# All work emitted by a list scheduler in the kernel, with tiles of its own for attention

## The chip, the cores and the metric

One core of a Trainium2 chip. The metric is device time in microseconds of one execution of the whole program; lower is better. The kernel before takes 993.18 us (median of 3 runs, 992.31 to 993.94).

## The reference, cut to what matters

```python
def _attn_ref(q, k, v, g_norm):                 # 4 batches, 8 heads, 576 tokens, 64 wide
    kv = np.einsum('bhsd,bhse->bhde', k, v)
    out = np.einsum('bhsd,bhde->bhse', q, kv)
    rms = np.sqrt(np.mean(out * out, axis=-1, keepdims=True) + 1e-06)
    return out / rms * g_norm

def _moe_ref(x, w_a, w_b, w_out):               # x 2304 x 512, inner width 1536
    return (x @ w_a) * (x @ w_b) @ w_out

def _moe2_ref(x, w_gate, w_val, w_out):
    gate = 1.0 / (1.0 + np.exp(-(x @ w_gate)))
    return gate * (x @ w_val) @ w_out
```

Attention without softmax, then two expert layers on the 2304 tokens, all in float32. Weights arrive as float64 bits (64-bit words) and are made float32 on the chip.

## The kernel before, in words

**Attention.** There are 18 tiles of 128 tokens. For each of the 4 batches four loads bring keys and values, 20 matmuls give the product of keys and values for all heads (word K in the order FIRST), and two copies put it into a block-diagonal tile (V). For each tile of tokens: a load of queries (D), the product with the block-diagonal tile into a bank (O), a square on ScalarE and a sum on VectorE (S), the reciprocal root on GpSimd for three tiles at once (R, `powers`, a scale-and-add and a power instruction of 24 columns), the normalisation on VectorE (N), four transposes on TensorE (T) and a scaled copy into `part`, the transposed x (Y). Attention borrows tiles of the expert layers: query tiles lie in those of the gated product, squares and normalised tiles in those of the first products.

**Expert layers.** The tokens are cut into 3 blocks of 768 (j), the inner width into 6 passes of two slices u and v (q), and there are two layers (m): 36 groups (m, q, j). A product of a group is a 256 x 256 by 256 x 384 block product; of these 7 instead of 8 are made from sums and differences of the blocks of x and of the weights (`x_comb`, `w_sums`), and recombined behind TensorE (`after`). They are numbered 1 to 7, for u and v each. Every operand is split into a rounded high part (ScalarE) and the remainder, the low part (a subtraction on GpSimd, in some cases VectorE), and a product is three matmuls for each of two inner halves: six matmuls of 384 columns, called a slot here. The gated product of u and v then goes through `down`, eight slots for a group, whose results VectorE adds into `part` (in the first pass q = 0 they are copied instead, by ScalarE and VectorE in turn).

**x.** In pass q = 0 of each layer the seven x operands of a block are made (`x_comb`), kept in a ring `xr` of 6 tiles and stored to DRAM; in the later passes they are loaded back (`load_x`). The keys and values of attention use the same ring.

**Weights.** Of each slice three matrices (a, b, o) are loaded (ring of 2), made float32 in four stages (`w_float`: two ScalarE instructions, three VectorE instructions, one integer add on GpSimd), combined (`w_sums`) and split (`w_parts`) into rings of 3 (wp0 to wp3) and 4 (wo).

**What sets the order.** Each engine executes in the order in which instructions are emitted, and SP, which issues all DMAs, too. That order is written by hand. FIRST lists attention and the first weights, and stands whole ahead of the first product. Then a loop runs over the groups, and in each over 22 slots (SLOTS: fourteen products and eight d, the down products of the group before). After each product of v the next x is made or loaded (`next_x`), and `hooks` places weight work at fixed slot numbers.

Of the kernel before, what the change touches and what calls it, by code (L numbers as in the profile page):

```python
# [10 lines left out]
F32 = mybir.dt.float32  # L11
F32R = mybir.dt.float32r
# [28 lines left out]
TICKS = len(SLOTS)  # L41
ORDER = "1526743"

W_OF = {"1": (0, 0), "2": (0, 1), "5": (1, 0), "7": (1, 1), "6": (2, 0), "4": (2, 1), "3": (3, 0)}

FIRST = """
L00 L01 L02 L03 C D1 L10 L11 D3 H H K0 V0 L12 L13 O0 S0 O1 S1 wa0 O2 S2 R0 L20 L21 D5 L22 L23 O3 S3 wb0 K1 V1
D7 L32 L33 L30 L31 N0 N1 O4 S4 T0 N2 O5 S5 Y0 R3 T1 Y1 q0 T2 Y2 p00 O6 S6 D10 N3 p10 N4 O7 S7 T3 N5 Y3 K2 T4 Y4 T5 Y5 V2
O8 S8 R6 c wa1 p20 D13 c p30 c O9 S9 wb1 N6 N7 q1 K3 c O10 S10 N8 p01 T6 Y6 T7 Y7 c V3 O11 S11 R9 T8 Y8 c p11
D16 O12 S12 O13 S13 N9 N10 p21 N11 T9 Y9 O14 S14 R12 T10 Y10 T11 Y11 p31 D17 O15 S15 O16 S16 N12 N13 O17 S17 R15
T12 Y12 T13 Y13 N14 N15 T14 Y14 T15 Y15 N16 N17 T16 Y16 T17 Y17
"""
# [3 lines left out]
def attention_then_two_moes(  # L61
# [9 lines left out]
    V, A, G = nc.vector, nc.scalar, nc.gpsimd  # L71

    def pool(name, bufs, on=ctx, **kw):
        return on.enter_context(tc.tile_pool(name=name, bufs=bufs, **kw))

    one = pool("one", 1)
    xr = pool("xr", 6)
    wp = pool("wp", 3)
    wo_p = pool("wo", 4)
    w32_p = pool("w32", 2)  # L80
    raw_p = pool("raw", 2)
    cv = pool("cv", 2)
    tmp = pool("tmp", 2)
    tmp2 = pool("gf", 2)
    xs = pool("xs", 1)
    unit = pool("unit", 1)
    small = pool("small", 2)
    dram = pool("dram", 1, space=DRAM)
    ps_u = pool("ps_u", 1, space=PSUM)
    ps_o = pool("ps_o", 2, space=PSUM)  # L90
# [3 lines left out]
    mhalf = one.tile([P, 3 * H], F32, name="mhalf")  # L94

    part = [one.tile([P, 2, KC, N], F32, name=f"part{j}") for j in range(NJ)]


    def u_tile(tag, shape=(P, N), dtype=F32):
        n = int(np.prod(shape[1:]))  # L100
        t = unit.tile([P, max(n, 512)], dtype, tag=tag, name=tag)[:, :n]
        return t if len(shape) == 2 else t.rearrange("p (a n) -> p a n", a=shape[1])

    kvbd = [u_tile(f"c22{x}", (P, KC, P)) for x in "uv"]


    w_raw, w_32, w_sum, w_pt, wo_pt = {}, {}, {}, {}, {}

    w_order = [(0, "a"), (0, "b"), (1, "a"), (1, "b"), (0, "o"), (1, "o")]
    w_order += [(F, w) for F in range(2, 2 * NF) for w in "abo"]  # L110

    def load_w():
        if not w_order:
            return
        F, which = w_order.pop(0)
        raw = raw_p.tile([P, KC * P], U64, tag="raw", name="wraw")
        nc.sync.dma_start(out=raw, in_=w_all[F // NF, F % NF, "abo".index(which)])
        w_raw[F, which] = raw

    def w_float(F, which, stage):  # L120


        raw = w_raw[F, which]
        words = (raw[0] if isinstance(raw, tuple) else raw).bitcast(U32).rearrange("p (n c) -> p n c", c=2)
        low, up = words[:, :, 0], words[:, :, 1]
        if stage == 0:
            mag = cv.tile([P, KC * P], F32, tag="mag", name="w_mag")
            last = cv.tile([P, KC * P], I32, tag="last", name="w_last")
            A.activation(out=mag, in_=up.bitcast(F32), func=ACTF.Abs, scale=65536.0)  # L129
            A.activation(out=last, in_=low, func=ACTF.Copy, scale=2.0**-29)  # L130
            w_raw[F, which] = raw, mag, last
            return
        raw, mag, last = raw
        bits = mag.bitcast(U32)
        if stage == 1:
            V.tensor_scalar(out=mag, in0=mag, scalar1=LEAST, scalar2=MOST, op0=ALU.max, op1=ALU.min)  # L136
            V.tensor_scalar(out=bits, in0=bits, scalar1=3, scalar2=None, op0=ALU.logical_shift_left)  # L137
        elif stage == 2:
            V.scalar_tensor_tensor(  # L139
                out=bits, in0=up, scalar=0x80000000, in1=bits, op0=ALU.bitwise_and, op1=ALU.bitwise_or  # L140
            )
            load_w()
        else:
            if F not in w_32:
                w_32[F] = w32_p.tile([P, 3, KC * P], F32, tag="w32", name="w32")
            dst = w_32[F][:, "abo".index(which), :].bitcast(I32)
            G.tensor_tensor(out=dst, in0=mag.bitcast(I32), in1=last, op=ALU.add)  # L147
            del w_raw[F, which]

    def w_sums(F, stage):  # L150
        w = w_32[F]
        b2 = w[:, 1, 256:512]
        if stage == 0:
            t13 = tmp.tile([P, 512], F32, tag="tmp", name="t13")
            V.tensor_tensor(out=t13, in0=w[:, 1, :], in1=w[:, 0:2, 0:256], op=ALU.subtract)  # L155
            w_sum[F] = [t13]
        else:
            t13 = w_sum[F][0]
            t24 = tmp.tile([P, 512], F32, tag="tmp", name="t24")
            V.tensor_tensor(out=t24[:, 0:256], in0=b2, in1=t13[:, 0:256], op=ALU.subtract)  # L160
            V.tensor_tensor(out=t24[:, 256:512], in0=w[:, 0, 256:512], in1=t24[:, 0:256], op=ALU.subtract)
            w_sum[F].append(t24)

    def w_parts(F, i, stage, eng=G):

        if i == "o":
            src, n = w_32[F][:, 2, :], 512
        elif i == 0:
            src, n = w_32[F][:, 0, :], 512
        elif i == 3:  # L170
            src, n = w_32[F][:, 1, 256:512], 256
        else:
            src, n = w_sum[F][i - 1], 512
        if stage == 0:
            if i == "o":
                t = wo_pt[F] = wo_p.tile([P, 2, n], F32R, tag="wo", name="wo")
            else:
                t = w_pt[F, i] = wp.tile([P, 2, n], F32R, tag=f"wp{i}", name=f"wp{i}")
            A.activation(out=t[:, 0, :], in_=src, func=ACTF.Copy)  # L179
        else:  # L180
            t = wo_pt[F] if i == "o" else w_pt[F, i]
            eng.tensor_tensor(out=t[:, 1, :], in0=src, in1=t[:, 0, :], op=ALU.subtract)  # L182


    x_dram, x_in = {}, {}
    x_sum = {}

    def x_comb(g, i, eng):

        m, q, j = g  # L190
        x11, x12, x21, x22 = (part[j][:, t, c:c + 2, :] for t in (0, 1) for c in (0, 2))
        if i == "5":
            x_sum[0] = one_x("s12")
            V.tensor_tensor(out=x_sum[0], in0=x21, in1=x22, op=ALU.add)  # L194
        elif i == "6":
            V.tensor_tensor(out=x_sum[0], in0=x_sum[0], in1=x11, op=ALU.subtract)  # L196
        elif i == "7":
            x_sum[1] = one_x("s3")
            V.tensor_tensor(out=x_sum[1], in0=x11, in1=x21, op=ALU.subtract)
        elif i == "3":  # L200
            V.tensor_tensor(out=x_sum[0], in0=x12, in1=x_sum[0], op=ALU.subtract)  # L201
        src = {"1": x11, "2": x12, "4": x22, "7": x_sum.get(1)}.get(i, x_sum.get(0))
        t = x_in[g, i] = xr.tile([P, 2, 2, N], F32R, tag="xr", name="xst")
        A.activation(out=t[:, 0], in_=src, func=ACTF.Copy)  # L204
        eng.tensor_tensor(out=t[:, 1], in0=src, in1=t[:, 0], op=ALU.subtract)  # L205
        d = x_dram[m, j, i] = dram.tile([P, 4 * N], F32, name=f"x{m}{j}{i}")
        nc.sync.dma_start(out=d, in_=t.rearrange("p a c n -> p (a c n)").bitcast(F32))

    def one_x(name):
        return xs.tile([P, 2, N], F32, tag=name, name=name)  # L210

    def load_x(g, i):
        m, q, j = g
        t = x_in[g, i] = xr.tile([P, 2, 2, N], F32R, tag="xr", name="xin")
        nc.sync.dma_start(out=t.rearrange("p a c n -> p (a c n)").bitcast(F32), in_=x_dram[m, j, i])

    groups = [(m, q, j) for m in range(2) for q in range(NQ) for j in range(NJ)]
    x_order = [(g, i) for g in groups for i in ORDER]

    def next_x():  # L220

        if not x_order:
            return
        g, i = x_order.pop(0)
        if g[1]:
            load_x(g, i)
        else:
            x_comb(g, i, V if i in "62" else G)


    kvm, qt = {}, {}

    def load_kv(b, p):

        if b < 2 or p > 1:
            t = xr.tile([P, 4 * N], F32, tag="xr", name="kv")[:, :KJ * 2 * P]
        else:
            t = part[b - 1][:, p].rearrange("p k n -> p (k n)")[:, :KJ * 2 * P]
        nc.sync.dma_start(out=t[:KP], in_=kv_in[b, p])
        kvm[b, p] = t[:KP].rearrange("p (j c e) -> p j c e", j=KJ, c=2)  # L240
# [310 lines left out]
```

## Time and profile before

| what | value |
| --- | --- |
| median of 3 runs | 993.18 us (992.31 to 993.94) |
| the profiled execution's own time | 991.95 us |
| its span | 990.1 us, 14127 instructions |
| TensorE matmul busy | 903.9 us, 91% of the span |
| VectorE (DVE) busy | 581.2 us, 59% |
| ScalarE (ACT) busy | 414.0 us, 42% |
| GpSimd (POOL) busy | 474.0 us, 48% |
| DMA | 256.78 MB, mean 259 GB/s |

How to read it: the span is the profiled execution from its first to its last instruction; its own time contains what lies around the span. Busy shares are means over stages that differ, so the rows below go by stages. In a timeline a row is a start, a duration, the engine, the line of the kernel, the instruction with output and inputs, and in brackets the idle time before it and what ended it. PE is TensorE, DVE is VectorE, ACT is ScalarE, POOL is GpSimd. PEclk is the granted clock as a share of the full one.

### The profile page before, as it was taken

The numbers are of one execution on the slowest core, as the hardware profiler recorded it, in microseconds if no ns is written. First come the engines' busy times: TensorE is split into PE (matmuls) and PEld (weight loads), VectorE is DVE, ScalarE is ACT, GpSimd is POOL, SyncE is SP. The second block draws the span as 40 slices with busy tenths as digits, with TensorE's granted clock in tenths as the row PEclk, the third lists the DMA queues.
The fourth block names the chain that finished last, engine by engine and source line by source line (L and its number), as shares of the span: only waits on it lengthen the run. The fifth ranks groups of instructions, "written<-read, shape, count | busy, mean of one in ns | idle before, by whom it ended". The sixth has DMA issues, their size and how long they took to land.

```text
span 990.1 us, 14127 instructions
## 1 busy us (share of the span) xinstructions
PE 903.9 (91%) x5144; PEld 890.9 (90%) x5144; DVE 581.2 (59%) x989; ACT 414.0 (42%) x805; POOL 474.0 (48%) x387
## 2 busy tenths in 40 slices
PE   6645677899999999999999798999999999999998
PEld 5544667899999999999999787999999999999998
DVE  2373388556566556656657868446566656664444
ACT  2244445453333333433434654554543444543321
POOL 2466377544454344444446786444444444544111
PEclk9777788999999999999999989899999999999999
DMA  8752255787887788778875646788778877877783
GB/s 335 291 202 107 117 190 214 287 305 274 281 310 282 282 290 304 273 263 297 306 270 217 235 193 236 264 313 301 273 259 317 284 272 274 302 268 246 248 275 119
DMA packets 55221, 256.78 MB, mean 259 GB/s; under 512 B 6256, under 2 KB 9328, under 8 KB 55152
## 3 DMA queue, kind: packets, MB, share of 16 engines
q1 hardware_dynamic: 55152, 255.88, 71.1%
q8 instruction: 41, 0.67, 0.3%
q14 instruction: 28, 0.23, 0.1%
HBM read 218.10 MB, written 37.75 MB: 258 GB/s over the span
## 4 chain that ended last, share of the span: by engine, by line
PE 76%; DVE 5%; ACT 2%; issue 1%; POOL 1%; DVEq 0%; ACTq 0%
PE ps_u L330 48%; PE ps_o L379 29%; ACT xst L204 1%; DVE w_mag L139 1%; DVE s L194 1%; POOL xst L205 1%; DVE s L196 1%; DVE w_mag L137 0%; DVE w_mag L136 0%; DVE s L201 0%; ACT w_mag L129 0%; DVE part L390 0%; DVE xst L205 0%; POOL w L147 0%; DVE t L155 0%
## 5 line engine op out<-in xcount | busy, mean ns | idle before, releaser
L330 PE MATMUL ps_u<-xin,wp 128*128 128x384 f32 x2520 | 456.4, 334 | 0.0
L330 PEld LDWEIGHTS ps_u<-xin,wp 128*128 128x128 f32 x2520 | 438.6, 188 | 0.0
L379 PE MATMUL ps_o<-gu,wo 128*128 128x384 f32 x864 | 201.6, 341 | 24.7 <-ACT part L386 8.7
L379 PE MATMUL ps_o<-gv,wo 128*128 128x384 f32 x864 | 199.9, 339 | 0.0
L147 POOL TENSOR_TENSOR w<-w_mag,w_last 128x512 int32<-128x512 int32 x72 | 95.0, 1319 | 210.8 <-DVE w_mag L139 164.4
L390 DVE TENSOR_TENSOR part<-ps_o,part 128x384 f32<-128x384 f32 x240 | 131.1, 554 | 107.0 <-PE ps_o L379 106.9
L379 PEld LDWEIGHTS ps_o<-gu,wo 128*128 128x128 f32 x864 | 155.2, 191 | 31.0 <-DVE part L390 11.4
L379 PEld LDWEIGHTS ps_o<-gv,wo 128*128 128x128 f32 x864 | 157.0, 191 | 0.0
L369 POOL TENSOR_TENSOR gu<-gf,gu 128x384 fp32r<-128x384 f32 x72 | 74.6, 1036 | 145.7 <-ACT gu L368 143.8
L330 PE MATMUL ps_u<-xst,wp 128*128 128x384 f32 x504 | 100.8, 357 | 12.4 <-ACT u2u L339 6.7
L330 PEld LDWEIGHTS ps_u<-xst,wp 128*128 128x128 f32 x504 | 96.7, 206 | 13.7 <-ACT u2u L339 7.1
L182 POOL TENSOR_TENSOR wp<-t,wp 128x512 fp32r<-128x512 f32 x48 | 64.7, 1349 | 70.6 <-ACT wp L179 70.6
L368 ACT ACTIVATE gu<-gf 128x384 fp32r<-128x384 f32 x72 | 37.8, 525 | 131.1 <-DVE gf L366 131.1
L369 POOL TENSOR_TENSOR gv<-gf,gv 128x384 fp32r<-128x384 f32 x72 | 77.8, 1081 | 15.9 <-ACT gv L368 13.6
L139 DVE SCALAR_TENSOR_TENSOR w_mag<-wraw,w_mag 128x512 uint32<-128x512 uint32 x72 | 65.2, 906 | 1.2
L136 DVE TENSOR_SCALAR w_mag<-w_mag 128x512 f32<-128x512 f32 x72 | 40.7, 565 | 37.7 <-ACT w_mag L129 36.9
L349 DVE TENSOR_TENSOR c11u<-ps_u,vu 128x384 f32<-128x384 f32 x36 | 20.0, 556 | 57.7 <-PE ps_u L330 57.6
L368 ACT ACTIVATE gv<-gf 128x384 fp32r<-128x384 f32 x72 | 37.6, 523 | 38.3 <-DVE gf L366 36.5
L182 POOL TENSOR_TENSOR wp<-w,wp 128x512 fp32r<-128x512 f32 (+1 forms) x48 | 50.0, 1041 | 6.7 <-ACT wp L179 6.6
L339 ACT ACTIVATE u2u<-ps_u 128x384 f32<-128x384 f32 x36 | 17.6, 489 | 81.1 <-PE ps_u L330 81.1
L129 ACT ACTIVATE w_mag<-wraw 128x512 f32<-128x512 f32 x72 | 47.8, 664 | 6.9 <-DMA wraw<-w_all_dram 5.7
L130 ACT ACTIVATE w_last<-wraw 128x512 int32<-128x512 uint32 x72 | 48.1, 668 | 0.0
(82 smaller groups left out, 865.2 us busy)
## 6 DMA issues: line engine op xcount, KB each, us to landing
xin<-x SPq DMA_DIRECT2D x210, 768.0 KB, 5.6
wraw<-w_all_dram SPq DMA_DIRECT2D x72, 512.0 KB, 4.5
x<-xst SPq DMA_DIRECT2D x42, 768.0 KB, 3.5
kv<-kv_in_dram SPq DMA_DIRECT2D x12, 640.0 KB, 8.3
out_dram<-part SPq DMA_DIRECT2D x24, 192.0 KB, 1.9
part<-kv_in_dram SPq DMA_DIRECT2D x4, 640.0 KB, 7.9
gu<-q_t_dram SPq DMA_DIRECT2D x9, 256.0 KB, 7.5
gv<-q_t_dram SPq DMA_DIRECT2D x9, 256.0 KB, 6.1
```

The lines of the kernel that those rows point to most:

```text
L129: A.activation(out=mag, in_=up.bitcast(F32), func=ACTF.Abs, scale=65536.0)
L130: A.activation(out=last, in_=low, func=ACTF.Copy, scale=2.0**-29)
L136: V.tensor_scalar(out=mag, in0=mag, scalar1=LEAST, scalar2=MOST, op0=ALU.max, op1=ALU.min)
L139: V.scalar_tensor_tensor(out=bits, in0=up, scalar=0x80000000, in1=bits, op0=ALU.bitwise_and, op1=ALU.bitwise_or)
L147: G.tensor_tensor(out=dst, in0=mag.bitcast(I32), in1=last, op=ALU.add)
L182: eng.tensor_tensor(out=t[:, 1, :], in0=src, in1=t[:, 0, :], op=ALU.subtract)
L330: nc.tensor.matmul(out=o, lhsT=w[:, a, c], rhs=x[:, b, k, :], start=(i in "152" and k == 0 and (a, b) == (0, 0)), stop=(k == 1 and (a, b) ...
L349: V.tensor_tensor(out=t, in0=o, in1=val["v", uv], op=ALU.add)
L368: A.activation(out=p[:, 0, :], in_=gf, func=ACTF.Copy)
L369: G.tensor_tensor(out=p[:, 1, :], in0=gf, in1=p[:, 0, :], op=ALU.subtract)
L379: nc.tensor.matmul(out=o, lhsT=wo_pt[f_of(g, uv)][:, a, c], rhs=g_pt[g, uv, t][:, b, :], start=(uv, a, b) == mms[0], stop=(uv, a, b) == mm ...
L390: V.tensor_tensor(out=acc, in0=o, in1=acc, op=ALU.add)
```

## The change

All work is described first, as operations with an engine, a duration, the operations they come after, the buffers they need and a due time; `Plan.order` then runs a list scheduler over them in the building program (on the host, nothing of it on the chip), and the operations are emitted in the order of their starting times there. An engine that is free takes the ready operation with the earliest due time whose buffers have room. Due times come from the slots (the first is put at 38 us, one each 1.044 us), and are carried back along the operations. Low parts may go to GpSimd or VectorE, whichever takes them first. Attention has own tiles (`q`, `sq`, `xn`, `kvbd`) and takes the reciprocal root tile by tile; keys-times-values and the transposes of tiles 0 to 11 use the bank o1; tiles 12 to 17 use o0 and o1, so that the six product banks are free after tile 11. Rings: xr from 6 to 5, wo from 4 to 3, float weights 4 of 512 columns in place of 2 of 1536. What is computed stays the same. Cut to its core:

```diff
-FIRST = """
...
+RINGS = {"xr": 5, "wp0": 3, "wp1": 3, "wp2": 3, "wp3": 3, "wo": 3, "w32": 4, "raw": 2, "mag": 2, "last": 2, "tmp": 2,
+         "gf": 2, "q": 3, "xn": 2, "ss": 2, "rr": 2}
+ANY_ORDER = ("o0", "o1")
+    def order(self):
...
+        def room(o):
+            for tag, b in o["new"]:
+                ring = rings.setdefault(tag, [])
+                if tag not in ANY_ORDER and turn[tag][nxt[tag]] != b:
+                    return False
+                if len(ring) >= RINGS.get(tag, 1) and users[ring[0]]:
+                    return False
+            return True
...
+            for e in free_at:
+                if free_at[e] > t:
+                    continue
+                best = None
+                for o in ready[e]:
+                    if (best is None or o["due"] < best["due"]) and room(o):
+                        best = o
...
+                ns = best["ns"] * (0.55 if len(best["eng"]) == 2 and e == "DVE" else 1)
+                best["at"], best["on"] = t, e
+                done.append(best)
...
+    LO = ("POOL", "DVE")
...
+        op(("load", k), "SP", dma(512), load, new=[("raw", raw)], lag=2000)
+        op(m, "ACT", 670, mag, [("load", k)], [("mag", m)], [raw])
+        op(l, "ACT", 670, last, [("load", k)], [("last", l)], [raw])
+        op(("clamp", k), "DVE", 900, clamp, [m], uses=[m])
+        op(("sign", k), "DVE", 750, sign, [("clamp", k)], uses=[raw, m])
+        op(w, "POOL", 1400, rounded, [("sign", k), l], [("w32", w)], [m, l])
...
+        op(("xh", g, i), "ACT", act(n), hi, after, [("xr", xin)], uses)
+        op(("xl", g, i), LO, pool(n), lo, [("xh", g, i)], (), [xin, *uses])
+        op(("xd", g, i), "SP", dma(768), store, [("xl", g, i)], (), [xin], lag=2000)
...
+        op(("xh", g, i), "SP", dma(768), load, [("xd", (m, 0, j), i)], [("xr", xin)], lag=2200)
...
+        tag, ttag = f"u{t % 6}" if t < 12 else f"o{t % 2}", f"o{t % 2}" if t >= 12 else "o1"
...
+        op(q, "SP", dma(256), load, (), [("q", q)], lag=2000)
+        op(bank, "PE", 1000, mm, [q] + [("V", i, e) for i, _, _ in batches(t) for e in (0, 1)]
+           + ([('T', t - 2)] if t >= 12 + 2 else []), [(tag, bank)], [q])
+        op(sq, "ACT", 610, square, [bank], [("sq", sq)], [bank])
+        op(ss, "DVE", 720, mean, [sq], [("ss", ss)], [sq])
+        op(rr, "POOL", 1950, power, [ss], [("rr", rr)], [ss])
+        op(xn, "DVE", 720, norm, [rr], [("xn", xn)], [bank, rr])
+        op(tbank, "PE", 480, transpose, [xn], [(ttag, tbank)], [xn])
...
+        op((*me, i), "PE", 1044, mm, x_ready + [(*w, "h"), (*w, "l")] + [(*me, b) for b in before],
+           [(tag, bank)] if i in "152" else [], [w, xin] + ([] if i in "152" else [bank]), due, 250)
...
+        op((*name, "f"), "DVE", dve(N), product_of, after, [("gf", gf)], [bank, (me, other)], due + 2800)
+        op((*name, "h"), "ACT", act(N), hi, [(*name, "f")], [(f"g{uv}{t}", name)], [gf])
+        op((*name, "l"), LO, pool(N), lo, [(*name, "h")], (), [gf, name])
...
+        op(("sum", g, t, d), "ACT" if on_act else "DVE", act(N) if on_act else dve(N), evict, [bank] + before,
+           uses=[bank], due=due + 2000)
...
+    done = plan.order()
     with tc.manual_schedule():
...
-        for word in FIRST.split():
-            do(word)
...
+        for o in done:
+            o["fn"](ENG[o["on"]]) if len(o["eng"]) == 2 else o["fn"]()
```

## Rows read from the trace of the kernel before

**Rows 1.** Stages of the span; columns are named in the first line.
```profile
core 0: us, PE busy (x) PEld busy (x) DVE busy (x) ACT busy (x) POOL busy (x), PEclk, DMA share, GB/s
0.00:104.15 104.15, 58.33 (x393) 53.39 (x393) 44.04 (x65) 36.78 (x63) 50.67 (x37) 0.80 0.58 222
104.15:197.27 93.12, 70.73 (x350) 68.08 (x349) 61.45 (x78) 43.43 (x80) 59.69 (x40) 0.86 0.57 215
197.27:542.96 345.69, 344.64 (x1981) 343.04 (x1981) 213.71 (x392) 136.08 (x269) 161.51 (x142) 1.00 0.78 283
542.96:633.98 91.02, 77.51 (x398) 75.18 (x398) 62.15 (x84) 47.50 (x89) 61.09 (x42) 0.91 0.59 225
633.98:986.70 352.72, 352.61 (x2029) 351.25 (x2028) 199.26 (x372) 150.25 (x305) 141.05 (x128) 1.00 0.76 269
0.00:197.27 197.27, 129.06 (x740) 121.47 (x741) 105.50 (x143) 80.21 (x142) 110.35 (x77) 0.83 0.57 219
```

**Rows 2.** Chain that ended last, steady state: start us, us, what.
```profile
218.23 8.32 PE ps_u L330 x48
```

**Rows 3.** TensorE's timeline, attention and the first expert products.
```profile
64.52 1.11 PE L303 MATMUL ps_t<-ident,u2u 128*128 128x128 f32 x4 [7.17 <-DVE u2u L292]
104.15 9.71 PE L330 MATMUL ps_u<-xst,wp 128*128 128x384 f32 x48
120.59 9.65 PE L330 MATMUL ps_u<-xst,wp 128*128 128x384 f32 x46 [6.74 <-ACT u2u L339]
```

**Rows 4.** VectorE's timeline ahead of the transpose at 64.52.
```profile
56.62 2.10 DVE L205 TENSOR_TENSOR xst<-part,xst 128x768 fp32r<-128x768 f32 x1 [1.95 <-ACT xst L204]
61.57 2.17 DVE L139 SCALAR_TENSOR_TENSOR w_mag<-wraw,w_mag 128x512 uint32<-128x512 uint32 x1
63.77 0.69 DVE L292 TENSOR_TENSOR u2u<-ps_a,rr 128x512 f32<-128x512 f32 x1
```

**Rows 5.** GpSimd in 0 to 197.27, groups by line: powers and weights.
```profile
L287 POOL TENSOR_TENSOR rr<-var,mhalf 128x24 f32<-128x24 f32 x6 | 25.4, 4227 | 0.5
L147 POOL TENSOR_TENSOR w<-w_mag,w_last 128x512 int32<-128x512 int32 x12 | 16.4, 1364 | 23.1 <-DVE w_mag L139 23.1
L285 POOL TENSOR_SCALAR var<-ss 128x24 f32<-128x24 f32 x6 | 1.7, 282 | 24.0 <-DVE ss L280 23.8
```

**Rows 6.** GpSimd's timeline around the third power instruction.
```profile
51.96 4.17 POOL L287 TENSOR_TENSOR rr<-var,mhalf 128x24 f32<-128x24 f32 x1
56.08 1.83 POOL L205 TENSOR_TENSOR xst<-part,xst 128x768 fp32r<-128x768 f32 x1
```

**Rows 7.** TensorE's timeline, stage between the two expert layers.
```profile
556.71 0.95 PE L379 MATMUL ps_o<-gu,wo 128*128 128x384 f32 x3 [3.18 <-DVE part L390]
619.90 1.33 PE L379 MATMUL ps_o<-gu,wo 128*128 128x384 f32 x3 [3.70 <-ACT part L386]
```

**Rows 8.** Windows of 20 us: the first two, two with VectorE and GpSimd busy.
```profile
0.00:20.00 20.00, 12.42 (x92) 11.96 (x92) 3.68 (x7) 5.22 (x10) 1.24 (x9) 1.00 0.90 355
20.00:40.00 20.00, 10.05 (x75) 8.70 (x74) 9.84 (x18) 6.61 (x13) 13.12 (x7) 0.87 0.96 377
160.00:180.00 20.00, 18.96 (x109) 18.32 (x107) 18.67 (x23) 9.92 (x18) 14.46 (x11) 1.00 0.45 161
540.00:560.00 20.00, 16.82 (x90) 16.50 (x89) 15.83 (x20) 13.37 (x24) 18.87 (x12) 0.93 0.52 202
```

**Rows 9.** Line 205 and line 201: duration ns min/median/max.
```profile
L205 POOL TENSOR_TENSOR xst<-s,xst x18: 1801/1844/2252, 61.2 to 614.4; 128x768 fp32r<-128x768 f32 x18
L205 DVE TENSOR_TENSOR xst<-s,xst x6: 957/958/958, 69.0 to 598.7; 128x768 fp32r<-128x768 f32 x6
...
L201 DVE TENSOR_TENSOR s<-part,s x6: 948/1045/2585, 102.5 to 610.8; 128x768 f32<-128x768 f32 x6
```

**Rows 10.** DMA issues: out<-in, engine, op, xcount, KB each, median us to landing.
```profile
xin<-x SPq DMA_DIRECT2D x210, 768.0 KB, 5.6
```

**Rows 11.** Groups by line, whole span: the evictions of the down products.
```profile
L390 DVE TENSOR_TENSOR part<-ps_o,part 128x384 f32<-128x384 f32 x240 | 131.1, 554 | 107.0 <-PE ps_o L379 106.9
```

More of the change, by code (lines that the diff above doesn't have):

```diff
@@ L104, in attention_then_two_moes @@
[L104 to L138, printed above, removed]
+    plan = Plan()
@@ L139, in w_float @@
             V.scalar_tensor_tensor(
-                out=bits, in0=up, scalar=0x80000000, in1=bits, op0=ALU.bitwise_and, op1=ALU.bitwise_or
+                out=m, in0=words(1), scalar=0x80000000, in1=m, op0=ALU.bitwise_and, op1=ALU.bitwise_or
             )
[L142 to L148, printed above, removed]
@@ L190, in x_comb @@
+    groups = [(m, q, j) for m in range(2) for q in range(NQ) for j in range(NJ)]
+    def x_comb(g, i, ready):
         m, q, j = g
         x11, x12, x21, x22 = (part[j][:, t, c:c + 2, :] for t in (0, 1) for c in (0, 2))
[L192 to L196, printed above, removed]
-        elif i == "7":
[L198 to L210, printed above, removed]
+        n = 2 * N
@@ new lines, in x_comb, with total, fn @@
+        xin, chain, s3 = ("x", g, i), ("s12", m, j), ("s3", m, j)
+        src = {"1": x11, "2": x12, "4": x22}.get(i)
+        after, uses = list(ready[i]), []
+        def total(name, tag, in0, in1, how):
+            def fn():
+                if name not in tl:
+                    tl[name] = new_tile(tag, [2, N])
+                V.tensor_tensor(out=tl[name], in0=tl[name] if in0 is None else in0,
+                                in1=tl[name] if in1 is None else in1, op=how)
+            return fn
@@ L218, in attention_then_two_moes @@
[L218 to L240, printed above, removed]
@@ L388, in down @@
                 V.tensor_copy(out=acc, in_=o)
-            return
-        V.tensor_tensor(out=acc, in0=o, in1=acc, op=ALU.add)
+        op(bank, "PE", 1044, mm, [(x, *n, e) for n in [("g", g, uv, t) for uv in "uv"] for x, *n in [n] for e in "hl"]
+           + [("wo", F, e) for F in fs for e in "hl"], [(tag, bank)],
+           [("wo", F) for F in fs] + [("g", g, uv, t) for uv in "uv"], due, 250)
+        before = [("sum", (m, q - 1, j), t, d)] if q else [("xl", g, i) for i in ORDER]
+        on_act = q == 0 and d % 2
@@ new lines, in attention_then_two_moes @@
+    x_ready = {}
+    at, prev = 38000, None
+    for n, g in enumerate(groups):
+        m, q, j = g
+        for i in ORDER:
+            if q:
+                x_ready[g, i] = load_x(g, i)
+            else:
+                blocks = {"1": (0,), "2": (0,), "4": (1,), "5": (1,)}.get(i, (0, 1))
+                if m == 0:
+                    after = [("Y", 6 * j + 3 * h + t) for h in blocks for t in range(3)]
+                else:
+                    after = [("sum", (0, NQ - 1, j), h, d) for h in blocks for d in range(KC)]
+                x_ready[g, i] = x_comb(g, i, {i: after})
+        k = 0
+        for slot in SLOTS:
+            if slot != "d":
+                product(n, g, slot[0], slot[1], x_ready[g, slot[0]], at)
+                if slot[0] == "7":
+                    total_5(g, slot[1], at + 3500)
+            elif prev is None:
+                continue
+            else:
+                down(prev, k, at)
+                k += 1
+            at += 1044
+        prev = g
@@ L488, in attention_then_two_moes @@
+    for k in range(2 * KC):
+        down(prev, k, at)
+        at += 1044
+    done = plan.order()
     with tc.manual_schedule():
-        warm = small.tile([P, 1], F32, tag="warm", name="warm")
+        warm = one.tile([P, 1], F32, name="warm")
         G.memset(warm, 0.0)
```

623 lines of the change are left out of this document (354 added, 269 removed).

## The prediction

> **What bounds the kernel now.** I read the table of stages first, then the chain that ended last, then the timelines of the places where TensorE stands still. The table [rows 1] cuts the span at five events: the first expert product (104.15 us), the first product on a reloaded x (197.27), the first product of the second layer (542.96), the first product on a reloaded x there (633.98), and the end of TensorE's work (986.7). The reader is to see that two of the stages are already full. From 197.27 to 542.96 TensorE is busy 344.64 of 345.69 us, from 633.98 to 986.7 it is busy 352.61 of 352.72, both at a granted clock of 1.00. In the chain 48 matmuls take 8.32 us there [rows 2], so one takes 173.3 ns, a slot of six 1.04 us, and a group of 22 slots 22.88 us; 15 groups are 343.2 us, and the stage took 345.7. No order of instructions can win more than about 2.5 us there.
>
> The other three stages are not full. Before 104.15 us TensorE is busy 58.33 us, at a granted clock of 0.80; the three groups behind it (14, 22 and 22 slots, 60.3 us at 1.04) take 93.12 us, so 32.8 are lost; the first three groups of the second layer (68.6 us) take 91.02, so 22.4 are lost [rows 1]. In all that is some 46 us of idle engine in the attention stage plus 55 in the other two.
>
> What makes it stand still is order. The transpose at 64.52 waited 7.17 us for a normalised tile [rows 3]. That tile's reciprocal root came from the power instruction that began at 51.96 and took 4.17 us [rows 6], so it was there at about 56.1. VectorE normalised only at 63.77, because a low part of x (2.10 us) and weight work (the last of it 2.17 us) stood ahead in its queue [rows 4]. None of that was due: the x tile and those weights serve a product that ran after 104 us. Behind it the written order lets no product start before tile 17 is transposed [rows 3]. In the stage between the layers, down products wait 3.18 and 3.70 us for an eviction that sits in VectorE's or ScalarE's queue behind work on x [rows 7].
>
> **The change part by part.**
> *Products beside attention.* Attention gets tiles and banks of its own, so a product of group 0 waits for tiles 0 to 5 and for its banks (the last of which tiles 6 to 11 hold), no longer for tile 17. TensorE's need up to 197.27 is at most 58.3 us of attention plus 60.3 of products, 118.6 in all, so TensorE would no longer set the end of this stage. What is late next is VectorE and GpSimd. They have 105.50 and 110.35 us there [rows 1], 215.9 together, and I treat them as one pair, since the change lets either take any low part.
>
> *The powers.* Six power instructions of 24 columns (4.23 us, and 0.28 for the one before) become 18 of 8 columns. No row shows 8 columns. If the time goes by columns, a tile costs 0.28 + 1.41 = 1.69 us, 30.4 in all against 27.1, +3.3. If it were fixed, 18 x 4.51 = 81 us, +54. I take the first, because the scale-and-add on the same 24 columns takes 0.28 [rows 5]: a 24-column instruction isn't dear by itself, the power is. Sum now 219 us; the other end stays in the range.
>
> *Low parts on either engine.* Without powers and their scale-and-add (27.1), the 12 integer adds of weights (16.4) [rows 5] and under 2 us of constants, GpSimd's low parts are about 65 us here. Nothing in the trace says what share the list gives to VectorE; the ends are none and all, and I take a third, since VectorE has as much other work as GpSimd. One of 768 columns takes 1.84 us on GpSimd and 0.96 on VectorE [rows 9], a saving of 0.48 of the time. A third of 65 saves 10.4: 208.6 us of work.
>
> *The pace of the pair.* In the first 40 us loads set it: DMA is 0.90 and 0.96 busy and the pair does 27.9 us of work [rows 8]. I leave that stretch as it is; the loads are the same and still needed first. For the other 180.7 us: between the layers the pair did 123.2 in 91.02 us, 1.35 per us [rows 1]; in its best 20 us windows 33.1 and 34.7, 1.66 and 1.73 [rows 8]. An order that always has something ready should come near the windows but not reach the best of them for a hundred microseconds, so I take 1.6: 113 us, and the stage ends at 153 instead of 197.3. The ends are 144 (at 1.73) and 181 (191 us of work with no low part moved, at 1.35).
>
> *Between the layers.* The same step: GpSimd's 61.09 us less six integer adds at 1.36 leave about 53 of low parts; a third moved saves 8.5; (123.2 - 8.5)/1.6 = 72 us in place of 91.0. The ends are TensorE's own 68.6 and today's 91.
>
> *The full stages.* The ring of x tiles goes from 6 to 5, of output weights from 4 to 3, and each weight's float form gets its own slot (4 of 512 columns in place of 2 of 1536). With five x tiles, a reload may begin when the fourth product pair before it starts; the shortest such stretch in the slot order is four pairs and one or two pairs of down products, 10 to 12 us, against 5.6 us from issue to landing [rows 10]. I cost it at nothing. The cover is that slack; a load later than it stops TensorE by the excess. SP's queue now holds loads and stores in the list's order, so a store that waits for a low part holds the x and weight loads behind it, by the same slack. The stages stay 346 and 353, the tail 3.4 (986.7 to 990.1) [rows 1].
>
> *Sum.* 153 + 346 + 72 + 353 + 3.4 = 927.4 us of span. The profiled execution took 991.95 for a span of 990.1, 1.85 outside it: 929 us against 992. The median of the runs shown is 1.2 above the profiled one, which is within what I can resolve.
>
> **The rivals.**
> *The pair blocks itself.* A subtraction of 768 columns on VectorE takes 948 ns at best and 2585 at worst [rows 9]; the one of 2.10 us lies beside a GpSimd low part that began at 56.08 [rows 4, 6]. If the two engines mostly exclude each other in this kind of work, a fuller order doesn't raise the pair's pace above the 1.35 between the layers, where both always had work. Then the first stage ends at 181 and the second stays at 91: 181 + 346 + 91 + 353 + 3.4 + 1.85 = 976. For it speaks that the list's durations know no such blocking; against it speak the windows of 1.66 and 1.73, and that many VectorE instructions read PSUM. [...]
>
> *The list doesn't overlap.* Banks of group 0 are free only once tiles 6 to 11 are normalised, keys-times-values and all early transposes share one bank, and x tiles come behind twelve key and value loads in one ring. If these keep products behind attention, the 104 us stay, and only the later losses shrink, by 13 and 19 us if the three groups take 80 and 72: 960.
>
> *Slower: evictions late in the full stages.* A bank of the down products is used again three slots (3.1 us) after it was filled; its eviction takes 0.55 [rows 11] and now stands in VectorE's queue among weight work and low parts in an order made with durations that know no blocking. The point from which it decides is 2.5 us of other work ahead of it. If each of the 144 pairs of down products then lost one such instruction, 0.55 us, that is 79 us: 929 + 79 = 1008. Against it: VectorE is busy only 213.7 of 345.7 us there, and evictions carry a due time near their product [rows 1].
>
> **How the numbers follow.** The forecast (914 to 955) has 0.60, its low end 144 + 344 + 69 + 352 + 3.4 + 1.85 = 914; better than that 0.04; the blocking pair (to 976) 0.15; no overlap 0.06; slower by late evictions 0.12; within 0.2% of now, gains and stalls cancelling, 0.03. A kernel whose powers don't shrink (+54 us of pair work, 34 us) would come to 963 and lies inside the range. The range 908 to 976 leaves out the slower case and little else. Faster by over 0.2% (about what a measurement of this kernel can tell from no change): 0.85; same 0.03; slower 0.12.
>
> **What would show it.** Right: expert products on the timeline from about 40 to 50 us, between transposes; the first reloaded x used at 145 to 165 us; low parts on VectorE; power instructions of about 1.4 us; the two full stages within 2 us of 346 and 353. The blocking pair shows as VectorE subtractions with a mean near 2 us and GpSimd busy all along while TensorE waits. Late evictions show as idle time of down products in the full stages, of which there is almost none now. Wrong would be my sum if the pair's total grows above 220 us, or if TensorE waits in the first stage for loads or banks while both engines idle.

## The result, and the profile after

The changed kernel takes 950.33 us (median of 4, 948.91 to 951.82) against 993.11: a ratio of 0.957, interval 0.955 to 0.959. That is 21 us above the 929 that I gave, inside the range of 908 to 976. The profiled execution took 950.53 us for a span of 948.7.

The stages of after, cut at the same five events as [rows 1], with the first three stages once more in the last row:

```profile
core 0: us, PE busy (x) PEld busy (x) DVE busy (x) ACT busy (x) POOL busy (x), PEclk, DMA share, GB/s
0.00:56.49 56.49, 40.57 (x289) 38.55 (x289) 32.17 (x47) 23.62 (x41) 30.09 (x35) 0.91 0.87 323
56.49:152.50 96.01, 81.08 (x455) 74.53 (x454) 86.27 (x119) 57.69 (x103) 67.30 (x51) 0.95 0.61 229
152.50:502.80 350.30, 347.98 (x1983) 346.81 (x1982) 254.68 (x456) 140.48 (x277) 126.45 (x102) 1.00 0.81 291
502.80:586.90 84.10, 75.49 (x397) 73.16 (x397) 77.31 (x99) 48.14 (x89) 49.62 (x30) 0.94 0.64 241
586.90:945.40 358.50, 356.45 (x2030) 355.06 (x2028) 234.07 (x417) 146.37 (x298) 87.55 (x74) 1.00 0.76 262
0.00:152.50 152.50, 121.65 (x740) 113.07 (x741) 118.44 (x165) 81.31 (x144) 97.39 (x85) 0.93 0.71 264
```

Against [rows 1] the reader sees three changes. Up to the first reloaded x the kernel needs 152.5 us instead of 197.3 (153 predicted). Between the layers it needs 84.1 instead of 91.0 (72 predicted), with VectorE busy 77.3 of them, 92%. The full stages have become longer, 350.3 and 358.5 instead of 345.7 and 352.7 (346 and 353 predicted), although TensorE waits 2 us in each. So TensorE itself is slower there. The miss is 12 us between the layers and 10 in the full stages.

The slower TensorE shows in the chain that ended last. Per pair of products (12 matmuls) and per two down products (12 matmuls) of after:

```profile
642.32 2.12 PE ps_u L494 x12
644.44 2.08 PE ps_o L586 x12
```

Before, both took 2.08 (48 in 8.32 in [rows 2], and in the same chain):

```profile
205.75 2.08 PE ps_u L330 x12
207.83 2.08 PE ps_o L379 x12
```

Single matmuls of the products now follow each other after 173 to 176 ns, with 180 to 182 in each fifth place, instead of 173.3; a group takes 23.13 us instead of 22.88.

Between the layers, from three timelines (start, duration, line): VectorE's queue, what lies beside it on GpSimd, and TensorE's wait behind them:

```profile
509.55 2.20 DVE L566 TENSOR_TENSOR gv<-gf,gv 128x384 fp32r<-128x384 f32 x1
511.68 2.60 DVE L307 TENSOR_TENSOR s<-part 128x768 f32<-128x768 f32 x1
514.20 0.55 DVE L517 TENSOR_TENSOR c11u<-ps_u,vu 128x384 f32<-128x384 f32 x1
514.67 0.94 DVE L329 TENSOR_TENSOR xr<-s,xr 128x768 fp32r<-128x768 f32 x1
516.00 0.54 DVE L594 TENSOR_TENSOR part<-ps_o,part 128x384 f32<-128x384 f32 x1
```

```profile
508.29 0.92 POOL L277 TENSOR_TENSOR wp<-w,wp 128x256 fp32r<-128x256 f32 x1
509.18 4.28 POOL L329 TENSOR_TENSOR xr<-part,xr 128x768 fp32r<-128x768 f32 x2
515.90 1.27 POOL L277 TENSOR_TENSOR wp<-tmp,wp 128x512 fp32r<-128x512 f32 x1 [2.44 <-ACT wp L273]
```

```profile
516.60 1.33 PE L586 MATMUL ps_o<-gu,wo 128*128 128x384 f32 x3 [3.10 <-DVE part L594]
```

While GpSimd does two low parts (509.18 to 513.46), VectorE's low part takes 2.20 us and its sum 2.60. Next to an idle GpSimd (513.46 to 515.90) a low part of the same size as the sum takes 0.94. The eviction that TensorE needs is late by about what the two were stretched, 3.3 us. The clock costs time as well. Behind the wait, groups of three matmuls start 0.96 us apart instead of 0.52: the granted clock is 0.50 from 515.8 to 522.6, and 1.00 before and after:

```profile
517.72 1.16 PE L586 MATMUL ps_o<-gv,wo 128*128 128x384 f32 x3
518.68 1.16 PE L586 MATMUL ps_o<-gu,wo 128*128 128x384 f32 x3
524.68 0.68 PE L586 MATMUL ps_o<-gu,wo 128*128 128x384 f32 x3
525.20 0.68 PE L586 MATMUL ps_o<-gv,wo 128*128 128x384 f32 x3
```

It falls to 0.50 once more, for 3.4 us at 546.5, behind a wait of 2.88. Of the 15.5 us that this stage takes above 68.6, TensorE is idle for 8.6; some 5 (half of 6.8 + 3.4) are matmuls at the clock of 0.50.

### The profile page after: what moved, and what is told of

Its sections match the earlier page's. It is cut to its first block, busy times and chain, and to the rows that moved or that the text cites. A ratio compares the mean times of both kernels' runs of the same rounds, so it can differ in the third digit from the quotient of the medians.

```text
span 948.7 us, 14074 instructions
## 1 busy us (share of the span) xinstructions
PE 901.6 (95%) x5144; PEld 888.1 (94%) x5144; DVE 685.0 (72%) x1135; ACT 416.3 (44%) x805; POOL 361.0 (38%) x289
## 4 chain that ended last, share of the span: by engine, by line
PE 73%; DVE 12%; POOL 5%; DMA 4%; issue 4%; ACT 1%; SPq 0%; POOLq 0%; ACTq 0%; DVEq 0%
PE ps_u L494 45%; PE ps_o L586 27%; DMA raw<-w_all_dram 3%; POOL rr L441 2%; DVE s L307 2%; DVE xr L329 1%; DMA xr<-kv_in_dram 1%; DVE mag L225 1%; DVE mag L231 1%; POOL w L237 1%; POOL xr L329 1%; PE ps_o L388 1%; DVE tmp L256 1%; DVE gf L559 1%; DVE part L594 1%
## 5 line engine op out<-in xcount | busy, mean ns | idle before, releaser
L494 PE MATMUL ps_u<-xr,wp 128*128 128x384 f32 x3024 | 561.9, 339 | 7.6 <-POOL xr L329 2.6
L494 PEld LDWEIGHTS ps_u<-xr,wp 128*128 128x128 f32 x3024 | 534.1, 188 | 11.5 <-POOL xr L329 3.2
L594 DVE TENSOR_TENSOR part<-ps_o,part 128x384 f32<-128x384 f32 x240 | 131.6, 553 | 70.8 <-PE ps_o L586 70.4
L237 POOL TENSOR_TENSOR w<-mag,last 128x512 int32<-128x512 int32 x72 | 102.4, 1429 | 69.0 <-DVE mag L231 54.9
L217 ACT ACTIVATE mag<-raw 128x512 f32<-128x512 f32 x72 | 47.8, 666 | 61.3 <-DMA raw<-w_all_dram 40.5
L225 DVE TENSOR_SCALAR mag<-mag 128x512 f32<-128x512 f32 x72 | 40.6, 563 | 29.2 <-ACT mag L217 29.2
L231 DVE SCALAR_TENSOR_TENSOR mag<-raw,mag 128x512 uint32<-128x512 uint32 x72 | 54.4, 756 | 0.8
L277 POOL TENSOR_TENSOR wp<-w,wp 128x256 fp32r<-128x256 f32 (+1 forms) x32 | 35.4, 1112 | 36.2 <-ACT wp L273 36.2
L221 ACT ACTIVATE last<-raw 128x512 int32<-128x512 uint32 x72 | 47.6, 662 | 0.0
L227 DVE TENSOR_SCALAR mag<-mag 128x512 uint32<-128x512 uint32 x72 | 44.1, 612 | 2.5
L566 DVE TENSOR_TENSOR gv<-gf,gv 128x384 fp32r<-128x384 f32 x44 | 35.2, 800 | 10.1 <-ACT gv L563 8.9
```

The source lines that it names most:

```text
L217: A.activation(out=tl["mag", k], in_=words(1).bitcast(F32), func=ACTF.Abs, scale=65536.0)
L221: A.activation(out=tl["last", k], in_=words(0), func=ACTF.Copy, scale=2.0**-29)
L225: V.tensor_scalar(out=m, in0=m, scalar1=LEAST, scalar2=MOST, op0=ALU.max, op1=ALU.min)
L231: V.scalar_tensor_tensor(out=m, in0=words(1), scalar=0x80000000, in1=m, op0=ALU.bitwise_and, op1=ALU.bitwise_or)
L237: G.tensor_tensor(out=tl["w32", k].bitcast(I32), in0=tl["mag", k].bitcast(I32), in1=tl["last", k], op=ALU.add)
L277: eng.tensor_tensor(out=t[:, 1, :], in0=tl[src][:, cut], in1=t[:, 0, :], op=ALU.subtract)
```

## The experiments

There are twelve runs, of eleven kernels. They answer three questions: did overlap win the first stage, why do matmuls of the products take 176 ns, and why did the stage between the layers shrink by 7 us only.

**Overlap.** e4 makes group 0 wait for all tiles, as the written order did (and tile 13 wait for the transpose of 11, which keeps the list from running out of banks):

```
-                    after = [("Y", 6 * j + 3 * h + t) for h in blocks for t in range(3)]
+                    after = [("Y", t) for t in range(NTILE)]
```

> The changed kernel, but the x operands of the first group wait for all 18 tiles of attention, as in the kernel before; the query product of tile 13 also waits for the transpose of tile 11. Theory A (the first stage is shorter because products run beside attention): first product at 80 to 100 us, first product on a reloaded x at 175 to 190 instead of 152.5, total 973 to 988. Theory B (the gain is the better order within attention and within the three groups): 155 to 162, total 952 to 960.

Measured: 981.23 us, ratio 0.988 (0.985 to 0.991); the first product at 112.0, later than the 80 to 100 expected, the first reloaded x at 184.6 instead of 152.5:

```profile
0.00:112.00 112.00, 65.77 (x393) 57.84 (x393) 59.87 (x98) 47.68 (x82) 58.81 (x62) 0.74 0.54 195
112.00:184.60 72.60, 66.70 (x348) 65.68 (x349) 63.06 (x78) 39.49 (x68) 42.58 (x24) 0.91 0.79 299
```

So 31 of the 43 us won are gone without products between the tiles. That is with the wait of tile 13, which no run has alone; the other 12 us were not taken apart. TensorE's granted clock is 0.74 in the first row, 0.91 and 0.95 in the two rows of after.

**The matmuls' period.** First guess: tiles that start off a multiple of 64 bytes. e1 widens the one tile ahead of the rings to 64 bytes; e2 puts 4 bytes into the kernel before, so that its rings lie 32 off.

> The changed kernel with one edit: the 4-byte tile warm, which lies ahead of all rings, is 64 bytes wide, so that every ring starts at a multiple of 64 bytes in SBUF and no longer 32 bytes beyond one. Theory A (the start address slows the products' matmuls): matmuls of the expert products come every 173.3 ns again instead of 173 to 182 (mean 176), a group in the full stages takes 22.88 us instead of 23.13, 36 groups give 9 us, total 941 (939 to 943). Theory B (the order or the semaphores around the products cause it): groups stay at 23.13, total 950 (948 to 952).

> The kernel before with one edit: a 4-byte tile is added behind the x accumulators, so that all rings start 32 bytes beyond a multiple of 64. Theory A (start address): groups go from 22.88 to 23.13 us, total 1002 (1000 to 1004). Theory B (order): nothing moves, 993 (992 to 994).

Measured: e1 950.23 (ratio 0.957, 0.955 to 0.959), groups 23.13, the same pattern. e2 993.22 (ratio 1.0004, 0.9992 to 1.0016), groups 22.88. The guess fell from both sides. What else the list had changed is where things lie: a ring and a PSUM bank are allotted at first use. e5 gives the banks in the order of before, e6 the rings:

```
+    for tag in ("xr", "wp0", "wp1", "wp2", "wp3", "wo", "w32", "raw", "mag", "last", "tmp", "gf"):
+        pools[tag] = ctx.enter_context(tc.tile_pool(name=tag, bufs=RINGS.get(tag, 1)))
```

> The changed kernel with its PSUM banks allotted as in the kernel before: the six banks of the products (u0 to u5) are banks 0 to 5 and the two of the down products (o0, o1) banks 6 and 7; in the changed kernel o1 is bank 0, u0 to u5 are banks 1 to 6 and o0 is bank 7, because a bank is allotted at its first use. Nothing else differs. Theory A (the changed kernel's products come every 176 ns instead of 173.3 because of the bank numbers): a group of the full stages takes 22.88 us again instead of 23.13, the gaps between matmuls of the products lose their pattern of 174, 175, 182, 175, 174 ns, and over some 31 groups the time falls by 8 us to 942. Theory B (the place of the x and weight tiles in SBUF) and theory C (neither): groups stay at 23.13 us and the time at 950, within 1 us.

> The changed kernel with its SBUF rings laid out in the order of the kernel before: x, weight parts 0 to 3, out parts, float weights, raw weights and so on, so that x lies at 58080 to 88800, the weight parts at 88800 to 131808 and the out parts at 131808 to 144096, nearly as in the kernel before; in the changed kernel a ring is laid out at its first use, and the weight parts lie at 125792 to 172896, the out parts at 203616. Theory B (the place of the tiles): groups take 22.88 us and the time falls by 8 us to 942. Theories A (banks) and C (neither): groups stay at 23.13 us, the time at 950 within 1 us.

Measured: e5 950.3 (ratio 0.958, 0.955 to 0.960), unchanged. e6 946.85 (ratio 0.953, 0.951 to 0.955), and its chain reads

```profile
642.08 2.08 PE ps_u L497 x12
644.16 2.12 PE ps_o L589 x12
```

The pattern had gone from the products to the downs. In after, x tiles start at 224 modulo 512 and weight parts at 352, while out parts and gated tiles both start at 352; in e6 x, weights and out parts start at 224 and gated tiles at 352. The pair that is 128 bytes apart is the slow one each time. The 128 bytes are the rings ss and rr, four tiles of 32. e8 lays them ahead of x; e9 sets other distances in the kernel before, 64 for the products and 256 for the downs:

```
+    for tag in ("ss", "rr"):
+        pools[tag] = ctx.enter_context(tc.tile_pool(name=tag, bufs=RINGS.get(tag, 1)))
```

> The changed kernel with the two rings of 32-byte tiles (ss and rr) laid out ahead of the x ring, so that every x, weight, out-part and gated tile starts at the same address modulo 512 bytes; in the changed kernel the x tiles lie at 224 modulo 512 and the weight parts at 352 (128 apart), the out parts and the gated tiles both at 352. Theory H (a matmul's period is 173.3 ns where its moving tile and its weights start at the same address modulo 512, and 176 ns on average where they are 128 apart; this fits the products and the downs of the kernel before, of the changed one and of the one with the rings in the order of before, where the pattern went from the products to the downs): products and downs both at 173.3 to 173.6 ns, groups of 22.88 us, the time 8 us shorter, 941 to 944. Rival (another effect of the order of the rings, as which lies next to which): products stay at 176 or the pattern turns up elsewhere; 946 to 951.

> The kernel before with 64 bytes of padding between its x ring and its weight parts, and 256 bytes more between its out parts and what lies behind, so that x and weights of the products are 64 apart modulo 512 and gated tiles and out parts of the downs 256 apart; nothing else differs. Theory H in its strict form (any distance modulo 512 other than 0 costs some 2.8 ns a matmul): products and downs at 176, groups of 23.2 us instead of 22.88, the time 11 to 12 us longer, 1004 to 1005. In a form modulo 256 the downs stay at 173.3, in a form modulo 64 or 128-byte lines the products do; then 7 us or 4 us longer, or no change. Rival (the distance is nothing): 993 within 1 us, all at 173.3.

Measured: e8 944.31 (ratio 0.951, 0.948 to 0.953), groups 22.88, no pattern left. e9 994.24 (ratio 1.002, 1.000 to 1.003), groups 22.91 in place of 22.88. Of e8, then of e9:

```profile
645.61 2.08 PE ps_u L497 x12
647.69 2.08 PE ps_o L589 x12
```

```profile
641.48 2.09 PE ps_o L381 x12
643.57 2.08 PE ps_u L332 x12
```

The time of e8 is just above the 941 to 944 expected. Its full stages:

```profile
152.20:502.60 350.40, 346.88 (x1981) 344.13 (x1980) 257.37 (x456) 140.86 (x277) 125.08 (x102) 1.00 0.82 291
586.50:940.90 354.40, 352.27 (x2029) 351.20 (x2028) 234.08 (x417) 146.47 (x298) 87.62 (x74) 1.00 0.78 264
```

The second is 4.1 us shorter than in after, the first isn't: its undisturbed groups are, but others took it back (TensorE is idle for 3.5 us of the stage, 2.3 in after).

So 6 us of the miss, by the medians, come from 128 bytes between moving tile and weights. The strict form of the theory fell: at 64 bytes nothing is lost, at 256 some 10 ns of a burst of 12. Why 128 costs is open, and no other distance was tried.

**Between the layers.** Theory of e3: the low parts that the list gives to VectorE are what is too much for it. e3 gives all to GpSimd (and has the same wait of tile 13 as e4):

```
-    LO = ("POOL", "DVE")
+    LO = ("POOL", "POOL")
```

> The changed kernel with low parts on GpSimd alone (the list may not give them to VectorE); the query product of tile 13 also waits for the transpose of tile 11, without which this list comes to no end. Theory A (the two engines take turns for work that reads SBUF twice, and a low part takes GpSimd 1.84 us against 0.96 on VectorE): the stage between the layers goes from 84 to 90 to 96 us, the first from 152.5 to 160 to 170, total 965 to 978. Theory B (VectorE, 92% busy between the layers, is simply overloaded, and the list gives it too much): the stage between the layers falls to 76 to 82, total 938 to 948.

Measured: 960.11, ratio 0.967 (0.965 to 0.969), between the two expectations, and by stage from the first reloaded x:

```profile
155.10:516.50 361.40, 351.03 (x1981) 347.99 (x1980) 246.91 (x416) 144.52 (x280) 181.25 (x154) 1.00 0.81 289
516.50:595.30 78.80, 72.93 (x398) 70.34 (x398) 59.45 (x80) 46.74 (x88) 70.58 (x45) 0.98 0.63 237
```

Between the layers 5 us were won, as theory B had it, in the first full stage 11 lost, a microsecond or more in about each third group. e7 tries the middle: VectorE takes a low part only where GpSimd is busy for another microsecond.

```
+                    if e == "DVE" and len(o["eng"]) == 2 and free_at["POOL"] < t + 1000:
+                        continue
```

> The changed kernel, whose list gives a low part to DVE only where POOL is busy for at least another 1 us (in the changed kernel DVE is asked first and takes every due low part for which it is free): 46 of the 306 low parts are on DVE instead of 134. Theory D (between the layers the low parts on DVE cost more there than they save on POOL, so DVE at 92% is the bound): the three groups between the layers take 74 to 80 us instead of 84.1, with DVE at 62 to 70 us busy; the first stage stays at 152.5 within 3 us; the full stages stay at 350 and 358 within 3; the time is 940 to 947. Theory E (the pair DVE and POOL has one pace, about 1.5 us of work per us, however the low parts are shared): between the layers 84 within 2, the time 949 to 952. Theory F (POOL's queue is what the full stages need relieved, as where all low parts are on POOL): the full stages become longer by up to 11 us, the time is 950 to 960.

Measured: 954.17, ratio 0.961 (0.959 to 0.962). Theory D fell by its own sum; the time is in the range of theory F. e12 is the same kernel once more, for its stages.

> The changed kernel whose list gives a low part to DVE only where POOL is busy for at least another 1 us (46 of 306 on DVE), once more, for its profile: it took 954.2 us where 940 to 947 was expected of theory D. Theory G (turns at SBUF): a low part holds SBUF for 1.0 to 1.9 us on POOL and for 0.55 to 0.95 on DVE, so that with more of them on POOL the DVE instructions without a PSUM operand stand longer: the loss against the changed kernel lies in the first stage and in waits in each third of the full stages' groups, with the group between the layers no shorter than 80 us. Theory F (POOL's own queue is what is late): the same groups are longer, but the waits end on POOL, and DVE's sums and clamps take no longer than in the changed kernel.

Measured: 953.98 in one execution.

```profile
0.00:160.20 160.20, 124.15 (x740) 115.88 (x741) 118.89 (x162) 82.56 (x147) 114.15 (x93) 0.90 0.68 249
513.00:592.40 79.40, 73.00 (x397) 70.46 (x396) 71.61 (x90) 46.24 (x87) 61.03 (x37) 0.98 0.65 248
```

Between the layers 79.4, the first stage 160.2 instead of 152.5. Here too moving low parts only moves the loss, and the 24 sums take 1.49 us on average, against 1.40 in after. That is for theory G, as is that TensorE waits longer for evictions on VectorE (11.4 us in all) than for low parts on GpSimd (3.6). "No shorter than 80" was missed by 0.6, and the second full stage, which was to lose, is 2.4 us shorter than in after.

The rows said why before a run did. In after the sums take (ns, min/median/max):

```profile
L307 DVE TENSOR_TENSOR s<-part x12: 943/1075/2614, 50.4 to 545.5; 128x768 f32<-128x768 f32 x12
L594 DVE TENSOR_TENSOR part<-ps_o,part x240: 541/551/560, 188.4 to 945.4; 128x384 f32<-128x384 f32 x120
```

In after no VectorE instruction with an operand in PSUM is stretched: the slowest of these 240 evictions takes 560 ns, and in no line with such an operand do the fastest and the slowest differ by more than 19 ns. A sum, with both inputs in SBUF, takes 0.94 us, or up to 1.7 more, which is nearly a whole low part of GpSimd (1.84). Beside a power it takes 0.94 us (VectorE's timeline, then GpSimd's):

```profile
84.65 0.94 DVE L307 TENSOR_TENSOR s<-s,part 128x768 f32<-128x768 f32 x1
```

```profile
84.27 1.64 POOL L441 TENSOR_TENSOR rr<-ss,mhalf 128x8 f32<-128x8 f32 x1
```

Theory G: in such work the two engines take turns, and the list doesn't know it. e10 leaves costs, due times and engines as they are (on the rings of e8) and only forbids the list to start such an instruction while the other engine is at one:

```
-                    if (best is None or o["due"] < best["due"]) and room(o):
+                    if (best is None or o["due"] < best["due"]) and not (
+                            o["sb"] and sb_end[OTHER[e]] > t) and room(o):
```

> The kernel with ss and rr ahead, and in the list a rule that an instruction of DVE all of whose operands are in SBUF (clamps, signs, sums, low parts) isn't started while POOL is at a low part or a rounding, nor the other way round; engines, costs and due times are as they were. Theory G (the two take turns at SBUF: in the changed kernel's trace such an instruction of DVE takes 0.95 us alone or beside a power and up to 2.61 beside a low part on POOL, one with a PSUM operand 0.55 always; the list doesn't know it, so its order leaves DVE standing 15 us between the layers): between the layers 69 to 77 us instead of 84.1, the first stage 138 to 150 instead of 152.5, no stray waits in the full stages; L307 at most 1.3 us on average instead of 1.3 to 1.9; the time 12 to 30 us below that of the kernel with ss and rr ahead alone, 912 to 930. Rival (the pair DVE and POOL is simply slower together, and order can't win it back): within 3 us of the kernel with ss and rr ahead alone, DVE still at 92% between the layers.

Measured: **914.94 us**, ratio 0.9205 (0.9189 to 0.922), 29 below e8. Its stages, and its sums (ns, min/median/max):

```profile
0.00:140.20 140.20, 115.63 (x740) 108.59 (x741) 100.01 (x161) 76.93 (x134) 74.75 (x70) 0.96 0.74 277
140.20:490.00 349.80, 345.91 (x1982) 344.66 (x1982) 247.07 (x461) 147.84 (x285) 136.40 (x115) 1.00 0.83 296
490.00:558.60 68.60, 68.60 (x397) 68.60 (x396) 58.12 (x86) 44.55 (x82) 36.88 (x25) 1.00 0.67 259
558.60:910.10 351.50, 351.50 (x2030) 351.36 (x2028) 223.47 (x425) 151.29 (x305) 98.61 (x87) 1.00 0.79 273
```

```profile
L315 DVE TENSOR_TENSOR s<-part x12: 944/950/2042, 48.7 to 525.0; 128x768 f32<-128x768 f32 x12
```

The loss between the layers is gone: TensorE is busy 68.60 of 68.60 us. The list put 131 low parts on VectorE (the 127 quoted below is a miscount), 134 in after, so the number on each engine isn't what changed. From the pages of e8 and of e10, the whole span:

```profile
PE 897.0 (95%) x5144; PEld 882.0 (93%) x5144; DVE 687.9 (73%) x1135; ACT 417.0 (44%) x805; POOL 359.7 (38%) x289
PE 881.9 (97%) x5144; PEld 873.2 (96%) x5144; DVE 629.2 (69%) x1132; ACT 420.6 (46%) x805; POOL 346.6 (38%) x292
```

VectorE and GpSimd together have 1424 instructions in both, busy 1047.6 us in e8 and 975.8 in e10. The work is the same but for three low parts that changed engine, so some 72 us of e8's busy time were instructions standing for the other engine. A part of the 29 us is the clock: between the layers it is 1.00 in e10, 0.94 in after and in e8. To tell the order from the sharing, e11 has the rule and all low parts on GpSimd (and, like e3 and e4, the wait of tile 13, which e10 hasn't):

> The kernel with ss and rr ahead and the rule of turns in its list, but all 306 low parts on POOL, as in the kernel before, where the list with the rule puts 127 of them on DVE (914.9 us). Theory G (the order that knows the turns is what counts): most of what the rule won is won here too, the time is 925 to 940, the three groups between the layers take 69 to 74 us, the full stages 343 to 348 and 352 to 354 without the 1 us that every third group lost where all low parts were on POOL and the list was blind to the turns; what is left above 914.9 lies in the first stage, where POOL has the powers too (155 to 165 us). Rival (the sharing of the low parts counts, and the rule only made it better): 950 to 956, which is the 960 of all low parts on POOL less some 6 us for the aligned rings, with waits in every third group as there.

Measured: 945.81, ratio 0.952 (0.949 to 0.956); the sum is between the two expectations. By stage:

```profile
0.00:156.30 156.30, 121.61 (x740) 114.19 (x741) 93.12 (x131) 75.79 (x133) 116.55 (x97) 0.91 0.67 245
156.30:194.50 38.20, 28.17 (x134) 26.37 (x133) 16.75 (x31) 14.44 (x29) 17.61 (x16) 0.87 0.65 231
515.70:584.40 68.70, 68.70 (x399) 68.70 (x398) 43.69 (x63) 41.72 (x77) 56.40 (x37) 1.00 0.62 238
```

Between the layers the rule alone is enough, and the losses of each third group are gone but for two of 0.6 and 0.2 us. What else was lost lies at the start: the first stage is 16 us longer than in e10, and the group behind it takes 38.2 us, where products wait up to 3.7 us for reloaded x tiles; the same group of the second layer takes 27.8. So between the layers the order counts; at the start the sharing seems to count too, but the wait of tile 13 is in those 16 us, and its part isn't known.

## Why the prediction was right, and where it wasn't

- *What bounds before* held: the full stages had nothing to give, the rest was order. e4 shows the largest part, overlap (with the wait of tile 13).
- *First stage.* 153 predicted, 152.5 measured, the pair's pace from 40 us on (215.8 - 33.0) / 112.5 = 1.62 against 1.6. The total of work, 215.8, is dearer than my 208.6: the powers cost 37.5 us with their scale-and-add, not 30.4, as 8 columns take 1.76 us and not 1.41:

```profile
L441 POOL TENSOR_TENSOR rr<-ss,mhalf 128x8 f32<-128x8 f32 x18 | 31.7, 1760 | 1.5
L439 POOL TENSOR_SCALAR ss<-ss 128x8 f32<-128x8 f32 x18 | 5.8, 325 | 22.7 <-DVE ss L435 21.4
```

  The stage came out right because the first 40 us did 33 us of work instead of 27.9. Two terms were off and made up for each other, by luck.
- *Between the layers: the step that failed.* "A third moved saves 8.5; (123.2 - 8.5)/1.6 = 72". Nothing was saved: the pair was busy 126.9 us, and its pace was 1.51. The sum took busy time for work that an order can't change, but it holds the time that one engine stands for the other, as e8 and e10 show. A low part on VectorE was priced at 0.96 us, its price beside an idle GpSimd; there low parts of 768 columns from the sums take 1.43 on average and those of 384 columns on VectorE 1.42 to 1.44:

```profile
L566 DVE TENSOR_TENSOR gv<-gf,gv 128x384 fp32r<-128x384 f32 x4 | 5.8, 1442 | 0.0
L329 DVE TENSOR_TENSOR xr<-s,xr 128x768 fp32r<-128x768 f32 x4 | 5.7, 1427 | 0.9 <-ACT xr L326 0.9
```

- *The pair blocks itself.* I gave this rival 0.15 and a price of 976, on the ground that the windows reach 1.66. The blocking is there: beside two low parts on GpSimd a low part on VectorE took 2.20 us and a sum 2.60 (509.55 and 511.68), and next to an idle GpSimd the fastest of their lines take 0.56 and 0.94. Not all work of GpSimd does it: a sum beside a power took 0.94 (84.65). Its price was wrong: the pair doesn't have one pace. VectorE's work with a PSUM operand isn't stretched beside GpSimd (L594: at most 560 ns), so the pace is a matter of which instructions the order puts side by side, and an order that knows it wins 29 us (e10 against e8). I had taken the blocking for a reason against the change; it was a reason against this list's durations.
- *Late evictions* happen where that rival's condition holds, two stretched instructions ahead of an eviction (516.60: 3.10 us), but more of them between the layers (6.5 us) than in the full stages (4.3). In all, TensorE's waits for L594 and L598 come to 12 us in after. My price for it, 79 us, counted the 144 pairs of all groups; the full stages have 124, 68 us.

```profile
PE ps_o L586 <- DVE part L594: 7.4, 5, 3.1
PE ps_o L586 <- DVE part L598: 4.7, 3, 2.9
```

- *The signs.* Reloaded x at 152.5 and low parts on VectorE came as named. Three others didn't: the first product came at 56.5, not at 40 to 50, a power takes 1.76 us, not 1.4, and the full stages are 4 and 5.5 us off, not within 2.
- *"I cost it at nothing"* (rings and full stages). The shorter rings cost nothing visible: no wait of TensorE for a reloaded x stands in after's view of waits. But a change of rings is also a change of addresses, and that cost 6 us, which no row of before could show.

The 21 us: some 12 between the layers, 6 by the addresses (e8), the rest stray waits such as 2.31 us at 189.04 for an eviction. The rule of e10 removes these from the second layer. In the first it leaves more of them than after has, in groups of 27.0, 24.2 and 24.0 us, where none was expected; in the first of these a product waits 2.29 us for a reloaded x at 150.98. Why is open.

## What to carry to other kernels

A list scheduler in a kernel is as good as its durations: where two engines exclude each other, put the exclusion into the list, not a mean price. The busy time of such an engine isn't its work, since it also holds the standing (the pair's 1047.6 us in e8 against 975.8 in e10). Look for one line whose fastest and slowest instruction differ by the length of another engine's instruction (here L307, 0.94 and 2.61 us; a low part on GpSimd takes 1.84). And after any change of buffers, compare the period of the matmuls (here 173 and 176 ns) before looking for waits.

## What the runs showed that I had not expected

- Matmuls whose moving tile and weights start 128 bytes apart modulo 512 came every 176.2 ns on average, with 180 to 182 in each fifth place (after, full stages, granted clock 1.00); at 0 (before) and 64 apart (e9) every 173.3, 48 in 8.32 us, and at 256 (e9) every 174.2, 12 in 2.09. It follows the tiles from the products to the downs, and depends neither on the PSUM banks (e5) nor on multiples of 64 (e1).
- A power on GpSimd of 8 columns takes 1.76 us against 4.23 for 24 ([rows 5]); a line through the two is some 0.5 us and 0.154 a column. No VectorE instruction that began inside one of after's 18 was stretched, sums and low parts of 768 columns included (0.94 to 0.96 us), although a power, too, has its operands in SBUF (`ss`, `mhalf`, `rr`).
